# Attention value products as two half-height products each, on one core

## The chip, the core and the metric

The kernel runs on one core of a Trainium2 chip. Its measure is the device time of one execution in microseconds. The matrix unit (TensorE, in the profile PE for products and PEld for loads of the stationary operand) takes the products; VectorE (DVE), ScalarE (ACT) and GpSimd (POOL) do the rest; SyncE (SP) issues the DMAs. Products land in PSUM, which has eight banks of 512 float32 columns in each of 128 partitions.

## The reference, cut to what is computed

```python
B, S, D, H, F = 1, 2048, 576, 32, 4608
xn = layernorm(x)                                   # no weights
q, k, v = split((xn @ wqkv), heads=32)              # 18 columns a head
p = softmax(q @ k.T * 18 ** -0.5)                   # 32 heads of 2048 x 2048
s = concat(p @ v) @ wo
g = silu((gelu(xn @ w_gate) * (xn @ w_up)) @ w_down)
out = x + s * g
```

Everything is float32. The products p @ v are the value products of this document.

## The kernel before, in words

A prologue normalises x and projects q, k and v into DRAM. Then one long loop runs attention and the feed-forward part side by side, and an epilogue applies `wo` and the gate. Most products take their operands as float32r (a high and a low part, several terms a product); the value products are plain float32, and the profile shows each of them as two loads and two products.

**Units.** Attention is cut into 128 sections. Four sections make one of `NU` = 32 units: a unit is four heads (`QD`) against one block of 512 queries (`TB`), and its section c takes keys of chunk c, 512 of them, as four tiles of 128 keys (kt). A section has first a mixed part: 27 pairs of gate and up products (`gate_up`, line 420), one of a pair in each half of the array's rows, so 64 rows each, and between them eight slots. A slot has a score pair of the current unit (`score_pair`, line 887, result `pe`), of which ScalarE makes exponentials into `pT` (line 888), and a pair for the maxima of the next unit (`max_pair`, line 846, result `pm`), which VectorE reduces (line 847, `mx`). Both are pairs of 64-row products too.

**Values.** Behind the mixed part `values` runs for the section's four key tiles (line 904). For each tile there are four products, one a head: 128 keys in rows, 32 columns of the stationary operand `VS` (18 values and a column of ones that gives the sum of the exponentials, the rest unused), 512 queries moving. The four heads lie in four column strips of the array, 32 wide, and land in four strips of 32 partitions of one bank. Chunk 0's result is copied into `accs` in SBUF by ScalarE (line 908); those of chunks 1, 2 and 3 are added to it by VectorE (line 910). After chunk 3 `accs` goes to DRAM, and a later section divides by the sums.

**Behind the values.** Behind chunk 2 of a unit VectorE ends the next unit's maxima (`max_parts`: `neg` of line 855, `mt` of line 858) and takes a reciprocal (line 935), and the next mixed part begins. Behind chunk 0 the next mixed part begins at once. Behind chunks 1 and 3 come the down products of the feed-forward part (`halved`, line 518, result `py`, 64-row pairs as well), which VectorE adds into `M` (line 568); then the next mixed part.

**PSUM.** All results of the loop share one ring of four tiles of two banks (`ring`, `RING` = 4). A section's `pgu` keeps one tile through its mixed part. The other three go round in the order of the program, so `pe` and `pm` take the tile of the third result before them: a `pm` takes that of the `pe` one slot before, a `pe` that of the `pm` two slots before, and the second `pe` of a section that follows values directly takes the tile of `acc`. A value result uses one of its tile's two banks.

**Order.** The order on TensorE is written out by hand (`spread` puts the slots between the pairs), as is SP's. VectorE, ScalarE and GpSimd are ordered by the scheduler in the loop, apart from instructions marked to stay in program order. Each engine runs its own list in order.

The epilogue's `project` (line 1059) and last down products (line 581) are products of 128 rows and 128 columns; between them lie gate and up pairs of 64 rows.

Of the kernel before, what the change touches and what calls it, by code (L numbers as in the profile page):

```python
# [8 lines left out]
F32 = mybir.dt.float32  # L9
F32R = mybir.dt.float32r  # L10
AF = mybir.ActivationFunctionType
ALU = mybir.AluOpType
# [5 lines left out]
P = 128  # L18
NT = S // P
TB = 512  # L20
# [3 lines left out]
HR = 64  # L24
# [3 lines left out]
QD = 4  # L28
# [5 lines left out]
NA = NS // SLOTS  # L34
VC = NT // NA
KB, VB = 7, 2
# [27 lines left out]
def part(b, r):  # L64
    return r if b != 1 or r > PLAIN else r - 1 if r > 0 else PLAIN
# [6 lines left out]
def f(ap):  # L72
    return ap.bitcast(F32)
# [14 lines left out]
def kernel(ctx: ExitStack, tc: tile.TileContext, x, wqkv, wo, w_gate, w_up, w_down, out):  # L88
    nc = tc.nc
# [83 lines left out]
    with tc.tile_pool(name="pro", bufs=1) as pro, tc.tile_pool(name="pps", bufs=1, space=PSUM) as pps:  # L173
# [120 lines left out]
        def split_qk(t, raw):  # L294
            hi, lo = (pro.tile([P, KT, P], F32R, name=f"q{m}{t}") for m in "hl")
            first = split(hi, lo, raw)
            put_qk(t, hi, lo)
            return first
# [31 lines left out]
        t = ORDER[0]  # L330
# [15 lines left out]
        last = norm(xr, 0, True, first_loads)  # L346
# [8 lines left out]
        for b in range(NB):  # L355
            if b == NB - 1:
                tc.keep_in_program_order(nc.scalar.activation(eps, eps, AF.Tanh))
            for n, t in enumerate(ORDER):
# [4 lines left out]
                if b == 0 and ahead_qk:  # L363
                    first = split_qk(*ahead_qk.pop(0))
# [40 lines left out]
    def ring(name):  # L405

        return ps.tile([P, 2, TB], F32, name=name, tag="ring", bufs=RING)
# [310 lines left out]
    def at(n, part, what, *args):  # L718
        todo.setdefault((n, part), []).append(lambda: what(*args))
# [66 lines left out]
    with tc.tile_pool(name="att", bufs=1, reuse_waits="tile") as att:  # L786
        VS = [att.tile([P, VC * VW + 32 - DH - 1], F32, name=f"VS{i}") for i in range(VB)]
# [36 lines left out]
        QS, MX, ACC, SUM, PT, NM, DEN = {}, {}, {}, {}, {}, {}, {}  # L824
# [12 lines left out]
        def max_pair(u, i):  # L837

            if u not in MX:
                MX[u] = att.tile([P, QD, 4, 4], F32, name="mx", bufs=2)  # L840
            i, r = divmod(i, 2)
            c, t = divmod(i, 4)
            pm = ring("pm")
            for a in range(2):
                rr = slice(HR * a, HR * a + HR)
                nc.tensor.matmul(pm[:, a], QS[u, r][rr, t * P:(t + 1) * P], KS[(u * NA + c) % KB][r][rr, :], start=True, stop=True)  # L846
            nc.vector.tensor_reduce(MX[u][:, 2 * r:2 * r + 2, t, c], pm, axis=AX.X, op=ALU.max)  # L847
# [4 lines left out]
        def max_parts(u):  # L852

            keep = tc.keep_in_program_order
            keep(nc.vector.tensor_reduce(NEG[:, 0].rearrange("p (a r t) -> p a r t", a=2, r=2),
                                         MX[u].rearrange("p (r a) t c -> p a r t c", a=2), axis=AX.X, op=ALU.max, negate=True))
            mt = att.tile([P, 8 * QD], F32, name="mt", bufs=2)
            keep(nc.vector.transpose(mt, NEG.rearrange("p z c -> p (z c)")))
            hl = NM[u] = att.tile([P, 2, 8 * QD], F32R, name="mhl", bufs=2)
            nc.scalar.activation(hl[:, 0], mt, AF.Copy)  # L860
            nc.gpsimd.tensor_tensor(hl[:, 1], mt, f(hl)[:, 0], op=SUB)
            FF["parts"] = True
            for i, part in ((9, max_store), (18, max_end)):
                FF["hooks"].setdefault(i, []).append(lambda part=part: part(u))
# [25 lines left out]
        def slot_pairs(s):  # L890

            um, im = divmod(s + LEAD, NS)
            return [lambda: score_pair(*divmod(s, NS))] + [lambda: max_pair(um, im)] * (um < NU)

        def values(u, kt):
            j, g = divmod(u, NQ)
            first, last = kt % VC == 0, kt % VC == VC - 1
            if first:
                ACC[u] = ring("acc")[:, 0]
            pt = PT.pop((u, kt))  # L900
            for a in range(QD):
                c, t = divmod(kt, VC)
                v = t * VW + (DH + 1) * a
                nc.tensor.matmul(ACC[u][32 * a:32 * a + 32, :], VS[(u * NA + c) % VB][:, v:v + 32], pt[:, a, :],  # L904
                                 start=first, stop=last, skip_group_check=True)
            if last and kt < VC:
                SUM[u] = att.tile([P, TB], F32, name="accs")
                nc.scalar.activation(SUM[u], ACC.pop(u), AF.Copy)
            elif last:
                nc.vector.tensor_tensor(SUM[u], ACC.pop(u), SUM[u], op=ALU.add)  # L910
            if kt == NT - 1:
                cols = slice(j * TB, (j + 1) * TB)
                acc = SUM[u]
                at(u * NA + NA - 1, 1, nc.sync.dma_start, oT[g, :, cols], acc)
                rt = rT[QD * g:QD * (g + 1), cols]
                if u < NU - 1:
                    todo.setdefault(((u + 1) * NA, 0), []).insert(0, lambda: sums(u, rt))
                    at((u + 1) * NA + 2, 2, reciprocals, u, rt)
                else:
                    at(NU * NA - 1, 2, last_sums, u, rt)  # L920

        def sums(u, rt):
            j, g = divmod(u, NQ)
            den = DEN[u] = att.tile([P, QD * TB // P], F32, name="sums", bufs=2)
            nc.sync.dma_start(den, oT[g].rearrange("(a p) t -> a p t", p=32)[:, 0, j * TB:(j + 1) * TB]
                              .rearrange("a (c s) -> a c s", s=QD * TB // P))
# [12 lines left out]
        for n, m in enumerate(FIRST):  # L939
            none = [lambda: None]  # L940
            lead = [lambda s=s: max_pair(*divmod(s, NS)) for s in range(slot, slot + m)]
            if m:
                lead = 5 * none + lead if n == 2 else 2 * none + lead + none
            section(lead)
            if slot + m >= NS > slot:
                max_parts(0)
            slot += m
            while n > 0 and chunk < KB and chunk * SLOTS <= slot + SLOTS:
                load_k(chunk)
                chunk += 1  # L950
            if n == 0:
                load_k(0)
                load_q(0)
            if n == 3:
                load_q(1)
            if n >= len(FIRST) - 2:
                load_v(n - len(FIRST) + 2)
            downs()
            finish()
        scaled = gated = 0  # L960
        later = {}
        for n in range(NU * NA):
            u, i = divmod(n, NA)
# [19 lines left out]
            for kt in range(i * SLOTS // 2, (i + 1) * SLOTS // 2):  # L983
                values(u, kt)
            if im == 0 and um <= NU:
                max_parts(um - 1)
# [11 lines left out]
    with tc.tile_pool(name="epi", bufs=1, reuse_waits="tile") as epi:  # L998
# [141 lines left out]
        first = FF["n"]  # L1140
# [27 lines left out]
        last = FF["raw"].pop(first + 4)  # L1168
# [9 lines left out]
        for m in ("rawd", "tsum"):  # L1178
            t = ffn.tile([P, 2, D], F32, name="xxs", tag=m)
# [34 lines left out]
        for i, c, m in QUARTERS:  # L1214
            t = ffn.tile([P, 2, DC], F32, name="tg", tag=("h0", "h1")[c], bufs=2 - c)
# [34 lines left out]
```

## Time and profile before

| | |
|---|---|
| median of 3 runs | 2528.89 us (2528.62 to 2529.62) |
| profiled execution, its own time | 2528.7 us |
| its span, first to last instruction | 2526.9 us |
| granted TensorE clock | 1.00 |
| TensorE busy | 2520.1 us (100%) |
| VectorE, ScalarE, GpSimd busy | 1890.4, 1666.2, 1599.4 us |
| value products on TensorE (line 904) | 466.0 us, 4096 of them |
| the loop with the values | from 317 to 2408 us of the span |

A row of a group gives the line, the engine, the operation, the tiles out<-in, the shapes and the count, then busy time in us and the mean of one in ns, then the idle time of that engine just before and who ended it. `64*128 64x512` is a stationary operand of 64 rows and 128 columns with 512 columns moving. A row of the timeline gives the start and the length in us of one or, with x2, of several instructions merged; a bracket at its end tells for how long the engine had been idle and who ended that. Lengths of products include what is in the pipeline, so it is the distance of starts that tells how fast they follow each other.

### The profile page before, as it was taken

The numbers are of one execution on the slowest core, as the hardware profiler recorded it, in microseconds if no ns is written. First come the engines' busy times: TensorE is split into PE (matmuls) and PEld (weight loads), VectorE is DVE, ScalarE is ACT, GpSimd is POOL, SyncE is SP. The second block draws the span as 40 slices with busy tenths as digits, with TensorE's granted clock in tenths as the row PEclk, the third lists the DMA queues.
The fourth block names the chain that finished last, engine by engine and source line by source line (L and its number), as shares of the span: only waits on it lengthen the run. The fifth ranks groups of instructions, "written<-read, shape, count | busy, mean of one in ns | idle before, by whom it ended". The sixth has DMA issues, their size and how long they took to land.

```text
span 2526.9 us, 58757 instructions
## 1 busy us (share of the span) xinstructions
PE 2520.1 (100%) x23434; PEld 1827.4 (72%) x23434; DVE 1890.4 (75%) x2085; ACT 1666.2 (66%) x1889; POOL 1599.4 (63%) x1652
## 2 busy tenths in 40 slices
PE   9999999999999999999999999999999999999999
PEld 8888866666766677666667666676666676666789
DVE  5326788888888888888887888888887788888247
ACT  3223377778777776777777777677777777777731
POOL 3005688888888875666657556566667666666773
PEclk9999999999999999999999999999999999999999
DMA  8965456555585566666677666666668666665766
GB/s 262 313 206 139 120 173 170 153 168 164 170 246 155 165 177 151 167 163 168 169 218 191 175 174 166 169 170 163 156 162 244 167 173 173 172 164 153 190 186 243
DMA packets 416649, 455.40 MB, mean 180 GB/s; under 512 B 109428, under 2 KB 289396, under 8 KB 416376
## 3 DMA queue, kind: packets, MB, share of 16 engines
q1 hardware_dynamic: 416376, 451.64, 65.1%
q8 instruction: 186, 3.05, 0.5%
q14 instruction: 87, 0.71, 0.1%
HBM read 354.38 MB, written 97.13 MB: 179 GB/s over the span
## 4 chain that ended last, share of the span: by engine, by line
PE 97%; DMA 2%; DVE 1%; POOL 0%; issue 0%; SPq 0%; ACT 0%; POOLq 0%; DVEq 0%
PE pgu L420 35%; PE acc L904 18%; PE py L518 16%; PE pm L846 10%; PE pe L887 9%; PE po L194 7%; PE po L1059 1%; DMA raw<-in_B_w_up_dram 1%; PE py L581 1%; PE pt L264 0%; DMA rT<-rec 0%; DMA xx<-in_A_wo_dram 0%; DMA T<-ts 0%; DMA xx<-in_A_x_dram 0%; DVE ol L1042 0%
## 5 line engine op out<-in xcount | busy, mean ns | idle before, releaser
L888 ACT ACTIVATE pT<-pe 128x1024 f32<-128x1024 f32 x1024 | 1048.6, 1027 | 469.4 <-PE pe L887 435.6
L847 DVE TENSOR_REDUCE mx<-pm 128x2 f32<-128x1024 f32 x1024 | 1218.7, 1226 | 143.9 <-PE pm L846 128.8
L420 PE MATMUL pgu<-xd,wh 64*128 64x512 f32 x5184 | 958.5, 393 | 0.0
L420 PEld LDWEIGHTS pgu<-xd,wh 64*128 64x128 f32 x5184 | 496.2, 184 | 122.5 <-issue 41.6
L118 POOL TENSOR_SCALAR wh<-raw 128x384 fp32r<-128x384 f32 x402 | 208.5, 519 | 506.7 <-PE pgu L420 264.0
L420 PE MATMUL pgu<-xd,wl 64*128 64x512 f32 x2592 | 514.4, 390 | 0.2 <-POOL wl L120 0.2
L904 PE MATMUL acc<-pT,VS 128*32 128x512 f32 x4096 | 466.0, 595 | 0.0
L120 POOL TENSOR_TENSOR wl<-raw,wh 128x384 fp32r<-128x384 f32 x402 | 407.4, 1014 | 33.0
L846 PE MATMUL pm<-KA,QT 64*128 64x512 f32 x2048 | 411.9, 396 | 0.2 <-DVE mx L847 0.2
L887 PE MATMUL pe<-QT,KA 64*128 64x512 f32 x2048 | 408.1, 391 | 0.0
L518 PE MATMUL py<-T,ah 64*128 64x288 f32 x3848 | 389.8, 294 | 0.0
L568 DVE TENSOR_TENSOR M<-py,M 128x576 f32<-128x576 f32 x448 | 333.2, 756 | 54.7 <-PE py L518 39.9
L518 PEld LDWEIGHTS py<-T,ah 64*128 64x128 f32 x3848 | 317.6, 184 | 53.2 <-issue 52.8
L441 POOL TENSOR_TENSOR al<-h,ah 128x512 fp32r<-128x512 f32 (+1 forms) x143 | 295.6, 2067 | 49.2 <-ACT ah L438 24.0
L904 PEld LDWEIGHTS acc<-pT,VS 128*32 128x32 f32 x4096 | 120.0, 109 | 276.9 <-issue 229.8
L518 PE MATMUL py<-T,al 64*128 64x288 f32 x1924 | 294.9, 291 | 0.0
L420 PEld LDWEIGHTS pgu<-xd,wl 64*128 64x128 f32 x2592 | 247.6, 184 | 46.6 <-POOL wl L120 0.6
L887 PEld LDWEIGHTS pe<-QT,KA 64*128 64x128 f32 x2048 | 192.9, 184 | 112.0 <-DVE mx L847 12.5
L432 DVE TENSOR_TENSOR h<-h,pgu 128x512 f32<-128x512 f32 x139 | 95.6, 687 | 194.2 <-ACT h L429 190.1
L846 PEld LDWEIGHTS pm<-KA,QT 64*128 64x128 f32 x2048 | 195.1, 184 | 55.5 <-ACT pT L888 15.8
L518 PEld LDWEIGHTS py<-T,al 64*128 64x128 f32 x1924 | 192.2, 185 | 0.0
L429 ACT ACT_TABLE_LOAD x129 | 165.5, 1283 | 2.4
(151 smaller groups left out, 2138.4 us busy)
## 6 DMA issues: line engine op xcount, KB each, us to landing
T<-ts SPq DMA_DIRECT2D x98, 576.0 KB
KA<-qk SPq DMA_DIRECT2D x768, 72.0 KB
T<-ts SPq DMA_DIRECT2D x98, 432.0 KB
raw<-in_B_w_gate_dram SPq DMA_DIRECT2D x144, 288.0 KB
raw<-in_B_w_up_dram SPq DMA_DIRECT2D x144, 256.0 KB
ts<-T SPq DMA_DIRECT2D x36, 576.0 KB
VS<-vs SPq DMA_DIRECT2D x128, 152.0 KB
qk<-t SPq DMA_DIRECT2D x72, 256.0 KB
```

The source lines that it names most:

```text
L118: first = nc.gpsimd.tensor_scalar(hi, raw, 1.0, 1.0, op0=ALU.mult, op1=ALU.mult)
L120: keep(nc.gpsimd.tensor_tensor(lo, raw, f(hi), op=ALU.subtract))
L194: nc.tensor.matmul(o, st, m, start=(i == 0), stop=(i == len(terms) - 1))
L420: nc.tensor.matmul(o, w[1 + wp][k][rr, c, :], xd[k][xp][rr, c, :], start=(i == 0), stop=(i == len(terms) - 1))
L441: low = two.tensor_tensor(lo, raw, f(hi), op=ALU.subtract)
L518: one = nc.tensor.matmul(py[:, t, 0:DC], h[rr, a, t * P:(t + 1) * P], T[rr, w, k], start=x == 0 and n == 0, stop=x == 1 and n == len(terms ...
L568: nc.vector.tensor_tensor(M[:, m], py[:, :, 0:DC], M[:, m], op=ALU.add)
L846: nc.tensor.matmul(pm[:, a], QS[u, r][rr, t * P:(t + 1) * P], KS[(u * NA + c) % KB][r][rr, :], start=True, stop=True)
L847: nc.vector.tensor_reduce(MX[u][:, 2 * r:2 * r + 2, t, c], pm, axis=AX.X, op=ALU.max)
L887: nc.tensor.matmul(pe[:, a], KS[(u * NA + c) % KB][r][rr, t * P:(t + 1) * P], QS[u, r][rr, :], start=True, stop=True)
L888: nc.scalar.activation(PT[u, kt][:, 2 * r:2 * r + 2, :], pe, AF.Exp, scale=SCALE)
L904: nc.tensor.matmul(ACC[u][32 * a:32 * a + 32, :], VS[(u * NA + c) % VB][:, v:v + 32], pt[:, a, :], start=first, stop=last, skip_group_chec ...
```

## The change

Each value product is cut in two: rows 0 to 63 of the keys and rows 64 to 127, each a product of 64 rows in its half of the array (`HR` = 64). The first half sums into the first bank of the ring tile, the second half into the second bank, so `acc` uses both banks and the array tile is 64x32 where it was 128x32. `accs` holds both sums, 1024 columns. Chunk 0 copies both at once on ScalarE; chunks 1 and 2 add both at once on VectorE. At the first key tile of chunk 3 VectorE joins the two sums in SBUF into one, and at chunk 3's end it adds the two banks to it, one after the other. To make room in SBUF, the maxima (`mx`) and their parts (`mhl`) have one buffer in place of two.

```diff
-                MX[u] = att.tile([P, QD, 4, 4], F32, name="mx", bufs=2)
+                MX[u] = att.tile([P, QD, 4, 4], F32, name="mx")
...
-            hl = NM[u] = att.tile([P, 2, 8 * QD], F32R, name="mhl", bufs=2)
+            hl = NM[u] = att.tile([P, 2, 8 * QD], F32R, name="mhl")
...
             if first:
-                ACC[u] = ring("acc")[:, 0]
+                ACC[u] = ring("acc")
+            if kt == NT - VC:
+                nc.vector.tensor_tensor(SUM[u][:, 0], SUM[u][:, 0], SUM[u][:, 1], op=ALU.add)
             pt = PT.pop((u, kt))
+            c, t = divmod(kt, VC)
             for a in range(QD):
-                c, t = divmod(kt, VC)
                 v = t * VW + (DH + 1) * a
-                nc.tensor.matmul(ACC[u][32 * a:32 * a + 32, :], VS[(u * NA + c) % VB][:, v:v + 32], pt[:, a, :],
-                                 start=first, stop=last, skip_group_check=True)
+                for half in range(2):
+                    rr = slice(HR * half, HR * half + HR)
+                    nc.tensor.matmul(ACC[u][32 * a:32 * a + 32, half], VS[(u * NA + c) % VB][rr, v:v + 32], pt[rr, a, :],
+                                     start=first, stop=last, skip_group_check=True)
             if last and kt < VC:
-                SUM[u] = att.tile([P, TB], F32, name="accs")
+                SUM[u] = att.tile([P, 2, TB], F32, name="accs")
                 nc.scalar.activation(SUM[u], ACC.pop(u), AF.Copy)
+            elif last and kt < NT - 1:
+                nc.vector.tensor_tensor(SUM[u], ACC.pop(u), SUM[u], op=ALU.add)
             elif last:
-                nc.vector.tensor_tensor(SUM[u], ACC.pop(u), SUM[u], op=ALU.add)
+                SUM[u], acc = SUM[u][:, 0], ACC.pop(u)
+                for half in range(2):
+                    nc.vector.tensor_tensor(SUM[u], acc[:, half], SUM[u], op=ALU.add)
```

## The prediction, as it was put on record

> **What bounds the kernel now.** I read the page first: busy shares, the chain of work that ended last, and the costliest groups.
>
> ```profile
> PE 2520.1 (100%) x23434; PEld 1827.4 (72%) x23434; DVE 1890.4 (75%) x2085; ACT 1666.2 (66%) x1889; POOL 1599.4 (63%) x1652
> ...
> PEclk9999999999999999999999999999999999999999
> ...
> PE 97%; DMA 2%; DVE 1%; POOL 0%; issue 0%; SPq 0%; ACT 0%; POOLq 0%; DVEq 0%
> PE pgu L420 35%; PE acc L904 18%; PE py L518 16%; PE pm L846 10%; PE pe L887 9%; PE po L194 7%; PE po L1059 1%; DMA raw<-in_B_w_up_dram 1%; PE py L581 1%; PE pt L264 0%; DMA rT<-rec 0%; DMA xx<-in_A_wo_dram 0%; DMA T<-ts 0%; DMA xx<-in_A_x_dram 0%; DVE ol L1042 0%
> ...
> L904 PE MATMUL acc<-pT,VS 128*32 128x512 f32 x4096 | 466.0, 595 | 0.0
> ```
>
> TensorE is the bound at full clock: 97% of the chain, and the value products (line 904) are 18% of it. So I went to the timeline of TensorE around one of their 128 runs, which shows where time in them is not streaming.
>
> ```profile
> 1209.77 0.41 PE L846 MATMUL pm<-KA,QT 64*128 64x512 f32 x2
> 1210.01 0.42 PE L420 MATMUL pgu<-xd,wh 64*128 64x512 f32 x2
> 1210.35 3.64 PE L904 MATMUL acc<-pT,VS 128*32 128x512 f32 x32
> 1213.92 0.50 PE L420 MATMUL pgu<-xd,wh 64*128 64x512 f32 x2
> 1214.26 0.39 PE L887 MATMUL pe<-QT,KA 64*128 64x512 f32 x2
> 1214.49 0.39 PE L420 MATMUL pgu<-xd,wl 64*128 64x512 f32 x2
> ```
>
> A pair of 64-row products normally starts 0.23 to 0.24 us after the pair before (1209.77 to 1210.01, 1214.26 to 1214.49). Into the values it is 0.34, out of the values the second pair is at 0.34 too (1213.92 to 1214.26). Inside the run, the weight loads and the length of one product give the rounds:
>
> ```profile
> 1210.81 0.13 PEld L904 LDWEIGHTS acc<-pT,VS 128*32 128x32 f32 x4 [0.30 <-issue]
> 1211.24 0.13 PEld L904 LDWEIGHTS acc<-pT,VS 128*32 128x32 f32 x4 [0.30 <-issue]
> ...
> L904 PE MATMUL acc<-pT,VS x4096: 592/592/617, 317.0 to 2408.0; 128*32 128x512 f32 x196
> ```
>
> The run ends at 1213.99 and its last product lasts 0.592, so that one starts at 1213.40. Four heads work side by side, a round takes 0.43 (1210.81 to 1211.24), and 32 products make eight rounds. After the last round the next pair would be due at 1213.40 - 0.02 + 0.43 = 1213.81; it starts at 1213.92. So one trip into the values and back costs 0.10 at the entry, 0.02 in the first round (its products are those of 617 ns instead of 592), 0.11 at the exit and 0.11 at the pair behind: 0.34 us, 43.5 us over 128 trips. That is all the change can gain on TensorE.
>
> Is this price one of the rows or of the columns? Only rows change at two places near the end, to 128x128 products and back:
>
> ```profile
> 2462.24 0.39 PE L420 MATMUL pgu<-xd,wl 64*128 64x512 f32 x2
> 2462.47 0.39 PE L420 MATMUL pgu<-xd,wh 64*128 64x512 f32 x2
> 2462.79 0.40 PE L1059 MATMUL po<-woh,oh 128*128 128x288 f32 x1
> 2463.03 0.30 PE L1059 MATMUL po<-wol,oh 128*128 128x288 f32 x1
> 2463.16 0.29 PE L1059 MATMUL po<-woh,ol 128*128 128x288 f32 x1
> ...
> 2449.62 0.29 PE L1059 MATMUL po<-wol,KA 128*128 128x288 f32 x1
> 2449.84 0.50 PE L420 MATMUL pgu<-xd,wh 64*128 64x512 f32 x2
> 2450.18 0.40 PE L420 MATMUL pgu<-xd,wl 64*128 64x512 f32 x2
> ```
>
> In: 0.32 instead of 0.23, then 0.24 instead of 0.13. Back: 0.22 instead of 0.13, then 0.34 instead of 0.23. That is 0.09 + 0.11 + 0.09 + 0.11 = 0.40 for a trip where rows alone change, not less than the 0.34 where rows and columns change at once.
>
> **The change part by part.** *Two products of 64 rows for each of 128.* A tile of 64x32 replaces one of 128x32; eight work side by side where four did. The pairs of halves in the rows above show that halves run beside each other: two products of 64 rows and 512 columns in 0.23. So I take a round as 0.43 still, eight rounds a run. From below it is that; from above, halves one after the other, eight rounds more, 128 x 8 x 0.43 = +440 us. The starts of one round are (0.13 - 0.109)/3 = 0.007 apart (load of 109 ns in the page's group of these loads, quoted below), so four more tiles in the last round let the next pair in 0.028 later: 128 x 0.028 = +3.6 us.
>
> *The switch.* Rows stay at 64 now, columns still go from 128 to 32 and back. No row of the trace shows a change of columns alone, so it costs between 0 and 0.34 a trip. The nearest rows are the two kinds of trip above: that a double change costs no more than a single one looks like one emptying of the array for any change of shape, not like a price of rows with columns free. I take the full 0.34: nothing gained. The Trainium skill, "TensorEngine Tiling (Array Packing)", under Key Properties, says that a change of the tiling mode, as against the tile, drains TensorE, and its list of configurations has 64x128 and 64x32 as two modes. By that rule the sum stays as I have it; the other reading is the first rival, and no run here shows a change of columns alone.
>
> *Emptying two banks.* Rows for the prices:
>
> ```profile
> L904 PEld LDWEIGHTS acc<-pT,VS 128*32 128x32 f32 x4096 | 120.0, 109 | 276.9 <-issue 229.8
> L910 DVE TENSOR_TENSOR accs<-acc,accs x96: 690/693/694, 334.5 to 2408.7; 128x512 f32<-128x512 f32 x96
> L568 DVE TENSOR_TENSOR M<-py,M 128x576 f32<-128x576 f32 x448 | 333.2, 756 | 54.7 <-PE py L518 39.9
> L888 ACT ACTIVATE pT<-pe 128x1024 f32<-128x1024 f32 x1024 | 1048.6, 1027 | 469.4 <-PE pe L887 435.6
> ```
>
> From 512 to 576 elements VectorE's add grows by 0.064 us, 0.001 an element, so an add of 1024 is 0.69 + 0.53 = 1.22 us. ScalarE's copy of 1024 is 1.03 as for the exponential of that size, against 0.60 for 512 (quoted below): +0.43. What this moves differs by chunk, of which a unit has four; there are 32 units.
>
> Chunk 2 is the dear one. VectorE's queue behind its add, and who waits for it:
>
> ```profile
> 1214.06 0.69 DVE L910 TENSOR_TENSOR accs<-acc,accs 128x512 f32<-128x512 f32 x1 [0.86 <-PE acc L904]
> 1214.67 0.21 DVE L855 TENSOR_REDUCE neg<-mx 128x16 f32<-128x64 f32 x1
> ...
> 1215.18 4.90 DVE L847 TENSOR_REDUCE mx<-pm 128x2 f32<-128x1024 f32 x4
> ...
> 1216.46 0.19 PEld L887 LDWEIGHTS pe<-QT,KA 64*128 64x128 f32 x2 [0.17 <-DVE mx L847]
> 1216.57 0.40 PE L887 MATMUL pe<-QT,KA 64*128 64x512 f32 x2
> ```
>
> The first reduction of the next section starts as soon as this queue lets it, at 1215.18, and takes 1.23. Of the four ring tiles one is held by pgu; the other three go round, so the third pe takes the tile of the first pm and its weight load follows that reduction's end (1216.41) by 0.05. With 0.53 more in front the reduction ends at 1216.94, the load is at 1216.99 and the product between 1217.00 (together with its load, as at 1213.92) and 1217.10 (0.11 behind it, as here): +0.43 to +0.53, I take 0.50. The products come in one order, so everything behind shifts and nothing wins it back.
>
> Chunk 0 is emptied by ScalarE:
>
> ```profile
> 1247.13 0.60 ACT L908 ACTIVATE accs<-acc 128x512 f32<-128x512 f32 x1
> ...
> 1247.83 2.12 ACT L888 ACTIVATE pT<-pe 128x1024 f32<-128x1024 f32 x2
> ...
> 1248.95 0.19 PEld L846 LDWEIGHTS pm<-KA,QT 64*128 64x128 f32 x2
> 1249.18 0.39 PE L846 MATMUL pm<-KA,QT 64*128 64x512 f32 x2
> ```
>
> The copy ends at 1248.16 instead of 1247.73, the first exponential 1.03 later at about 1249.19 instead of 1248.86. The second pm has that pe's tile: its load comes at 1249.24, the product at 1249.25 to 1249.35 instead of 1249.18: +0.07 to +0.17, I take 0.12.
>
> Behind chunks 1 and 3 the down products come, and VectorE has a gap before it adds the first:
>
> ```profile
> 1227.79 0.69 DVE L910 TENSOR_TENSOR accs<-acc,accs 128x512 f32<-128x512 f32 x1 [0.84 <-PE acc L904]
> 1229.15 3.14 DVE L568 TENSOR_TENSOR M<-py,M 128x576 f32<-128x576 f32 x4 [0.67 <-PE py L518]
> ```
>
> The 0.67 covers chunk 1's +0.53. Chunk 3's second add of 0.69 ends 0.02 late, which the four adds win back (3.14 for 4 x 0.756 = 3.02). If that cover went, the 0.53 and 0.69 would cost 39 us. The join of the two sums, one add of 512 (about 0.7), stands at the start of chunk 3's values, in front of the 0.84 that VectorE waits there. Nothing. The store of the sums through SP's queue leaves up to 0.7 later; what reads it back is taken a section later, at no price. One buffer in place of two for the maxima and their parts: their reader stands ahead of the next writer on VectorE already (1214.67 before 1215.18). Nothing.
>
> **Sum.** 32 x (0.50 + 0.12) + 3.6 = 23.4 us. The profiled execution took 2528.7 us (span 2526.9), 0.2 below the median of the runs shown, so 2552 us.
>
> **The rivals.** *Columns are free, rows were the price* (the other side). For it: every costly trip in the trace changes rows. Against: a double change costs no more than a single one. Place: both ends of each run of values. Gain in a unit: the entry, 4 x 0.12 = 0.48, and the exits behind chunks 1 and 3, 2 x 0.22 = 0.44. The exits behind chunks 0 and 2 bring nothing, since the waits there hang on the emptying, which counts from the end of the values. Against 0.62 + 4 x 0.028 = 0.73, net -0.19 x 32 = -6 us: 2523. It decides from four fifths of the price saved (0.73 of 0.92).
>
> *The switch gets cheaper by half*: -0.46 + 0.73 = +0.27 a unit, +9 us: 2538.
>
> *Columns free and the emptying hidden* (VectorE put the maxima before the adds): -43.5 + 3.6: 2489. Against: the queue order shown, in which the add is ready 1.1 us before the first maximum.
>
> *TensorE is not fed fast enough.* A round now has eight loads and eight products in 0.43. The densest stretch of today:
>
> ```profile
> 1228.14 0.44 PE L518 MATMUL py<-T,ah 64*128 64x288 f32 x4
> 1228.40 0.31 PE L518 MATMUL py<-T,al 64*128 64x288 f32 x2
> 1228.54 0.44 PE L518 MATMUL py<-T,ah 64*128 64x288 f32 x4
> ```
>
> Six products in 0.40, 0.066 each. Were that the limit of issue, a round would take 0.53: 8 x 128 x 0.10 = +102, and 2654 with the sum above. Against it: single 128x128 products of 288 columns also take 0.13 (2463.03 to 2463.16), so columns set that pace, not issue. The Trainium skill, "TensorE: Matmul & The Clock Gate", Part 1, gives about 62 ns a matmul when firmware decodes; by it a round would be an estimated 0.50, no run here tells how this chip decodes.
>
> **How the numbers follow.** Full price 0.44, half 0.10, columns free 0.30, free and hidden 0.09, fed too slowly (or halves one after another) 0.07. Range 2514 to 2560 leaves out the last two, 0.16. Its upper end is the full price with waits of 0.53 and 0.17 (2555) and 5 us for what I rounded, its lower end columns free with 0.43 and 0.07 (2519) and the same 5 us. The likeliest case alone spans 2544 (0.43, 0.07, no later start) to 2560. A measurement of this kernel tells about 0.2% (5 us) from nothing. Columns free lies at that edge: two thirds faster (0.21), with free and hidden 0.30. Same: the rest, and a little of half, 0.12. Slower 0.58.
>
> **What would show it.** Right: the first pair behind the values still 0.34 before the second; the entry still 0.34; eight rounds of 0.43; add 1.22 and copy 1.03; behind chunk 2 a weight load of the third pe that waits 0.4 to 0.6 for a maximum. Wrong: pairs at 0.23 on both sides of the values (columns free), rounds above 0.45 (feed), or maxima ahead of the adds on VectorE.

## The result, and the profile after

The changed kernel takes 2566.25 us (median of 4 runs) against 2529.26 for the kernel before: ratio 1.0145, 95% interval 1.0127 to 1.0163. It is slower, as forecast, by 37 us where 23 were forecast, and it lies 6 us above the range.

The page after, line by line against the one before (busy shares, the chain, the value products' group, then who keeps `pe` waiting):

```profile
PE 2536.7 (99%) x27530; PEld 1842.8 (72%) x27530; DVE 1959.2 (76%) x2149; ACT 1673.9 (65%) x1889; POOL 1599.7 (62%) x1652
...
PE 95%; DVE 4%; issue 1%; DMA 0%; ACT 0%; SPq 0%; DVEq 0%
PE pgu L420 33%; PE acc L908 18%; PE py L518 15%; PE pm L846 9%; PE pe L887 9%; PE po L194 7%; PE po L1067 2%; DVE accs L914 1%; DVE mx L847 1%; PE py L581 1%; PE pt L264 0%; DVE mt L858 0%; DVE accs L901 0%; DMA KA<-qk 0%; DMA xx<-in_A_x_dram 0%
...
L908 PE MATMUL acc<-pT,VS 64*32 64x512 f32 x8192 | 469.0, 592 | 0.0
...
L887 PE MATMUL pe<-QT,KA 64*128 64x512 f32 x2048 | 408.7, 396 | 21.4 <-DVE mx L847 21.4
```

Twice as many value products take 469.0 us of TensorE's time, where half as many took 466.0: eight tiles run beside each other, in rounds of 0.429 us as before. What is new is VectorE in the chain (4%, where it was 1%) with the lines of the emptying, the join (L901) and the maxima, and 21.4 us in which TensorE stands idle for a maximum. Before, the same row of `pe` had none:

```profile
L887 PE MATMUL pe<-QT,KA 64*128 64x512 f32 x2048 | 408.1, 391 | 0.0
```

The timeline of TensorE behind one chunk 2, after:

```profile
1225.14 0.40 PE L846 MATMUL pm<-KA,QT 64*128 64x512 f32 x2
1225.37 0.40 PE L420 MATMUL pgu<-xd,wh 64*128 64x512 f32 x2
1225.70 3.66 PE L908 MATMUL acc<-pT,VS 64*32 64x512 f32 x64
1229.30 0.49 PE L420 MATMUL pgu<-xd,wh 64*128 64x512 f32 x2
1229.63 0.40 PE L887 MATMUL pe<-QT,KA 64*128 64x512 f32 x2
...
1232.82 0.50 PE L887 MATMUL pe<-QT,KA 64*128 64x512 f32 x2 [0.63 <-DVE mx L847]
1233.15 0.39 PE L420 MATMUL pgu<-xd,wl 64*128 64x512 f32 x2
```

The entry is 0.33 (1225.37 to 1225.70), the second pair 0.33 behind the first (1229.30 to 1229.63): the price of the trip is all there, though rows no longer change. From the first value product to the first pair behind is 3.60, where it was 3.57: the later end of eight tiles. And the third `pe` of the section comes 3.52 after the first pair; before it was 2.65 (1213.92 to 1216.57). Behind its wait the next pair is 0.33 away as well (1232.82 to 1233.15), 0.10 more than usual.

To see where the 37 us lie, I took the distance from each run of values to the next and subtracted that of the kernel before, for the 32 units, by the chunk that stands ahead (median of one, and the sum):

| behind chunk | 0 | 1 | 2 | 3 |
|---|---|---|---|---|
| changed kernel, us each | +0.11 | +0.03 | +1.00 | +0.03 |
| sum, us | 3.5 | 0.8 | 32.6 | 1.5 |

The sum is 38.4, and the spans differ by 38.2 (2565.1 and 2526.9). Chunks 0, 1 and 3 did what the prediction said. Behind chunk 0 it is also the second `pm` that waits, for an exponential behind ScalarE's longer copy:

```profile
1263.59 1.03 ACT L912 ACTIVATE accs<-acc 128x1024 f32<-128x1024 f32 x1
...
1265.58 0.19 PEld L846 LDWEIGHTS pm<-KA,QT 64*128 64x128 f32 x2 [0.25 <-ACT pT L888]
```

Chunk 2 lost twice as much. VectorE's timeline there shows why:

```profile
1229.47 1.23 DVE L914 TENSOR_TENSOR accs<-acc,accs 128x1024 f32<-128x1024 f32 x1 [0.91 <-PE acc L908]
1230.61 0.21 DVE L855 TENSOR_REDUCE neg<-mx 128x16 f32<-128x64 f32 x1
1230.74 0.68 DVE L901 TENSOR_TENSOR accs<-accs 128x512 f32<-128x512 f32 x1
1231.34 0.20 DVE L858 STREAM_TRANSPOSE mt<-neg 128x32 f32<-128x32 f32 x1
1231.47 0.21 DVE L943 RECIPROCAL sums<-sums 128x16 f32<-128x16 f32 x1
1231.60 2.29 DVE L847 TENSOR_REDUCE mx<-pm 128x2 f32<-128x1024 f32 x2
```

The join L901, written at the start of chunk 3's values, does not run there. The scheduler, which orders VectorE in the loop, put it between `neg` and `mt`, one section earlier, where chunk 2's add has already made its operand. So two things stand ahead of the first maximum: the longer add (+0.53) and the join. The join takes 0.60 of the queue (1230.74 to 1231.34), but `mt` would have started only 0.24 behind `neg` without it (as in the next kernel below) and starts 0.73 behind it now, so it adds 0.49. The maximum starts 2.13 after the add (1229.47 to 1231.60), where it was 1.12, and the third `pe` waits for its end.

### The profile page after: what moved, and what is told of

Read it like the earlier page. It is cut to its first block, busy times and chain, and to the rows that moved or that the text cites. A ratio compares the mean times of both kernels' runs of the same rounds, so it can differ in the third digit from the quotient of the medians.

```text
span 2565.1 us, 67100 instructions
## 1 busy us (share of the span) xinstructions
PE 2536.7 (99%) x27530; PEld 1842.8 (72%) x27530; DVE 1959.2 (76%) x2149; ACT 1673.9 (65%) x1889; POOL 1599.7 (62%) x1652
## 3 DMA queue, kind: packets, MB, share of 16 engines
q8 instruction: 218, 3.57, 0.6%
## 4 chain that ended last, share of the span: by engine, by line
PE 95%; DVE 4%; issue 1%; DMA 0%; ACT 0%; SPq 0%; DVEq 0%
PE pgu L420 33%; PE acc L908 18%; PE py L518 15%; PE pm L846 9%; PE pe L887 9%; PE po L194 7%; PE po L1067 2%; DVE accs L914 1%; DVE mx L847 1%; PE py L581 1%; PE pt L264 0%; DVE mt L858 0%; DVE accs L901 0%; DMA KA<-qk 0%; DMA xx<-in_A_x_dram 0%
## 5 line engine op out<-in xcount | busy, mean ns | idle before, releaser
L908 PE MATMUL acc<-pT,VS 64*32 64x512 f32 x8192 | 469.0, 592 | 0.0
L887 PE MATMUL pe<-QT,KA 64*128 64x512 f32 x2048 | 408.7, 396 | 21.4 <-DVE mx L847 21.4
L120 POOL TENSOR_TENSOR wl<-raw,wh 128x384 fp32r<-128x384 f32 x402 | 407.5, 1014 | 33.3
L518 PEld LDWEIGHTS py<-T,ah 64*128 64x128 f32 x3848 | 309.5, 185 | 52.9 <-issue 52.8
L908 PEld LDWEIGHTS acc<-pT,VS 64*32 64x32 f32 x8192 | 141.3, 106 | 258.5 <-issue 211.5
L518 PE MATMUL py<-T,al 64*128 64x288 f32 x1924 | 285.9, 291 | 0.0
L518 PEld LDWEIGHTS py<-T,al 64*128 64x128 f32 x1924 | 184.0, 185 | 0.0
```

The source lines that it names most:

```text
L120: keep(nc.gpsimd.tensor_tensor(lo, raw, f(hi), op=ALU.subtract))
L518: one = nc.tensor.matmul(py[:, t, 0:DC], h[rr, a, t * P:(t + 1) * P], T[rr, w, k], start=x == 0 and n == 0, stop=x == 1 and n == len(terms ...
L887: nc.tensor.matmul(pe[:, a], KS[(u * NA + c) % KB][r][rr, t * P:(t + 1) * P], QS[u, r][rr, :], start=True, stop=True)
L908: nc.tensor.matmul(ACC[u][32 * a:32 * a + 32, half], VS[(u * NA + c) % VB][rr, v:v + 32], pt[rr, a, :], start=first, stop=last, skip_group ...
```

## The experiments

My theory after the result: a change of columns costs the full trip, and the rest is VectorE's queue ahead of the first maximum, half of it the misplaced join. The rivals are that something else in the change makes the loss (the single buffer of the maxima, the `acc` tile held longer, the 64-row products), or that columns are cheap and the emptying hides it. The kernel before, run beside them, takes 2529.86 us for the first four kernels and 2529.7 for the last two. "By chunk" is the loss of one section against the kernel before, as in the table above, behind chunks 0, 1, 2 and 3.

**The join where its line stands.** The join is held behind the last maximum of chunk 3's section (`behind` tells the scheduler the order of two instructions).

```diff
-            nc.vector.tensor_reduce(MX[u][:, 2 * r:2 * r + 2, t, c], pm, axis=AX.X, op=ALU.max)
+            FF["reduced"] = nc.vector.tensor_reduce(MX[u][:, 2 * r:2 * r + 2, t, c], pm, axis=AX.X, op=ALU.max)
...
-                nc.vector.tensor_tensor(SUM[u][:, 0], SUM[u][:, 0], SUM[u][:, 1], op=ALU.add)
+                behind(nc.vector.tensor_tensor(SUM[u][:, 0], SUM[u][:, 0], SUM[u][:, 1], op=ALU.add), FF["reduced"])
```

> The changed kernel with the join of the two sums held behind the last maximum of chunk 3's section, where its line stands in the text. My theory: of the 1.00 us lost behind each chunk 2, about half is the join, which the scheduler put between neg and mt, in front of the first maximum; the rest is the add's 0.53. So behind chunk 2 the loss falls from 1.00 to about 0.50, all else stays (0.11 behind chunk 0, 0.03 behind 1 and 3): 2529 + 32 x (0.50 + 0.11 + 0.06) = about 2550 us. Rival: the loss is made by the single buffer of the maxima and their parts, or by the acc tile that the second pe waits for; then 1.00 stays and the time is 2566.

Measured: 2549.87 us, ratio 1.0079 (1.0066 to 1.0091). By chunk +0.12, +0.02, +0.53, +0.03. VectorE behind chunk 2, and the third `pe`'s load:

```profile
1222.57 1.22 DVE L914 TENSOR_TENSOR accs<-acc,accs 128x1024 f32<-128x1024 f32 x1 [0.90 <-PE acc L908]
1223.71 0.21 DVE L855 TENSOR_REDUCE neg<-mx 128x16 f32<-128x64 f32 x1
1223.95 0.21 DVE L858 STREAM_TRANSPOSE mt<-neg 128x32 f32<-128x32 f32 x1
1224.09 0.21 DVE L943 RECIPROCAL sums<-sums 128x16 f32<-128x16 f32 x1
1224.21 2.29 DVE L847 TENSOR_REDUCE mx<-pm 128x2 f32<-128x1024 f32 x2
...
1225.43 0.19 PEld L887 LDWEIGHTS pe<-QT,KA 64*128 64x128 f32 x2 [0.58 <-DVE mx L847]
```

The first maximum now starts 1.64 after the add, and the join is hidden. One instruction's place in a queue is worth 16 us of the 37. The single buffers are still there, so they are not the cause of these 16. This kernel is the change as I had costed it; its time is 2 us below my 2552.

**The end of the maxima ahead of chunk 2's values.** In addition, `max_parts` is called before the values and not behind them.

```diff
+            if im == 0 and um <= NU:
+                max_parts(um - 1)
             for kt in range(i * SLOTS // 2, (i + 1) * SLOTS // 2):
                 values(u, kt)
-            if im == 0 and um <= NU:
-                max_parts(um - 1)
```

> The kernel late_join with the end of the next unit's maxima (neg, mt) put ahead of chunk 2's values, so that they run while VectorE waits for the values. The add of 1024 columns stays as long as it is. My theory (what counts is only what stands in VectorE's queue between the values' end and the first maximum): the first maximum starts about 0.15 later than in the kernel before instead of 0.53, the loss behind chunk 2 falls to 0.1 to 0.2, and the time is 2529 + 32 x (0.15 + 0.11 + 0.06) = about 2539 us. Rival (the acc tile is held longer, and the second pe waits for it): the add ends at the same time as in late_join, so the loss stays about 0.5 and the time is 2550.

Measured: 2540.37 us, ratio 1.0042 (1.0029 to 1.0055). By chunk +0.12, +0.02, +0.18, +0.03.

```profile
1217.51 0.21 DVE L855 TENSOR_REDUCE neg<-mx 128x16 f32<-128x64 f32 x1
1217.76 0.21 DVE L858 STREAM_TRANSPOSE mt<-neg 128x32 f32<-128x32 f32 x1
1218.50 1.23 DVE L914 TENSOR_TENSOR accs<-acc,accs 128x1024 f32<-128x1024 f32 x1 [0.53 <-PE acc L908]
1219.64 0.24 DVE L943 RECIPROCAL sums<-sums 128x16 f32<-128x16 f32 x1
1219.80 4.84 DVE L847 TENSOR_REDUCE mx<-pm 128x2 f32<-128x1024 f32 x4
```

The add is as long as before and ends as late behind the values (1.33 behind the end of the last value product in both kernels, median), so the `acc` tile is held as long; yet most of the loss is gone, since the first maximum starts 1.30 after the add and not 1.64. The second `pe`'s load does wait for the tile, but for the same 0.23 in the kernel with only the join late (the first row) and in this one (the second):

```profile
1223.85 0.19 PEld L887 LDWEIGHTS pe<-QT,KA 64*128 64x128 f32 x2 [0.23 <-DVE accs L914]
...
1219.78 0.19 PEld L887 LDWEIGHTS pe<-QT,KA 64*128 64x128 f32 x2 [0.23 <-DVE accs L914]
```

So what made the difference is the queue ahead of the maximum, not the hold of the tile.

**Chunk 0 by two engines.** In addition, ScalarE copies the first bank and VectorE the second.

```diff
-                nc.scalar.activation(SUM[u], ACC.pop(u), AF.Copy)
+                nc.scalar.activation(SUM[u][:, 0], ACC[u][:, 0], AF.Copy)
+                nc.vector.tensor_copy(SUM[u][:, 1], ACC.pop(u)[:, 1])
```

> The kernel late_join_early_max with chunk 0 emptied by two engines at once, ScalarE the first bank and VectorE the second. My theory: ScalarE's copy takes 0.60 again, so the 0.08 that chunk 0 loses beyond the later start of eight tiles goes: 2 to 3 us less than late_join_early_max, about 2536 us, and what is left over the kernel before is the later end of eight tiles, 128 x 0.03. Rival (the change of columns is cheaper than I think and the emptying hid it): with the emptying hidden the time falls below the kernel before, to 2520 or less.

Measured: 2542.99 us, ratio 1.0052 (1.0039 to 1.0064): slower than the kernel before it by 2.6, not faster by 2 to 3. Behind chunk 0 it loses 0.19 where that lost 0.12. The timeline behind one chunk 0, ScalarE, VectorE and the loads:

```profile
1253.50 0.60 ACT L912 ACTIVATE accs<-acc 128x512 f32<-128x512 f32 x1
...
1254.13 0.69 DVE L913 COPY accs<-acc 128x512 f32<-128x512 f32 x1 [1.54 <-ACT accs L912]
...
1254.87 0.19 PEld L887 LDWEIGHTS pe<-QT,KA 64*128 64x128 f32 x2 [0.33 <-DVE accs L913]
```

The two copies do not run at once: VectorE's waits for ScalarE's (1.54 idle, ended by the ACT line), though it reads another bank. The tile is then free at 1254.82, and the second `pe`, which takes it, waits for that. My expectation was wrong in this step. The two copies share the ring tile that they read and the `accs` tile that they write; which of the two orders them, no run here shows. As the emptying is not hidden behind chunk 0, this kernel is no test of cheap columns there. Behind chunks 1 and 3, where the emptying costs nothing in any of these kernels, cheap columns would have been a gain, and the sections lose 0.03 as in the others.

**One bank emptied.** All 64-row products run, but the second half's sums and the join are left out.

```diff
-            if kt == NT - VC:
-                nc.vector.tensor_tensor(SUM[u][:, 0], SUM[u][:, 0], SUM[u][:, 1], op=ALU.add)
...
-                SUM[u] = att.tile([P, 2, TB], F32, name="accs")
-                nc.scalar.activation(SUM[u], ACC.pop(u), AF.Copy)
-            elif last and kt < NT - 1:
-                nc.vector.tensor_tensor(SUM[u], ACC.pop(u), SUM[u], op=ALU.add)
+                SUM[u] = att.tile([P, TB], F32, name="accs")
+                nc.scalar.activation(SUM[u], ACC.pop(u)[:, 0], AF.Copy)
             elif last:
-                SUM[u], acc = SUM[u][:, 0], ACC.pop(u)
-                for half in range(2):
-                    nc.vector.tensor_tensor(SUM[u], acc[:, half], SUM[u], op=ALU.add)
+                nc.vector.tensor_tensor(SUM[u], ACC.pop(u)[:, 0], SUM[u], op=ALU.add)
```

> The changed kernel's products, but only the first bank is emptied: the second half's sums are left out, and the join with them. TensorE does all that the changed kernel does, VectorE and ScalarE what the kernel before does. My theory: the products cost only the later end of eight tiles, 128 x 0.03, so 2529 + 4 = about 2533 us. Rival A (columns free, hidden by the emptying): 2490 to 2520. Rival B (64-row products of plain float32 or their second bank slow other work): above 2538.

Measured: 2534.11 us, ratio 1.0016 (1.0007 to 1.0025): 4.2 us. By chunk +0.05, +0.03, +0.05, +0.03. On TensorE the change gains nothing and costs little more than the later end of eight tiles. So 33 of the 37 us are the emptying and the join.

**Values without a change of shape.** On top of it, a section's values are products of 64x128 tiles: as many rounds, one head's worth of products in place of four, other columns of `VS`.

```diff
-            for a in range(QD):
-                v = t * VW + (DH + 1) * a
-                for half in range(2):
-                    rr = slice(HR * half, HR * half + HR)
-                    nc.tensor.matmul(ACC[u][32 * a:32 * a + 32, half], VS[(u * NA + c) % VB][rr, v:v + 32], pt[rr, a, :],
-                                     start=first, stop=last, skip_group_check=True)
+            for half in range(2):
+                rr = slice(HR * half, HR * half + HR)
+                nc.tensor.matmul(ACC[u][:, half], VS[(u * NA + c) % VB][rr, 0:P], pt[rr, t, :],
+                                 start=first, stop=last, skip_group_check=True)
```

> The kernel one_bank, but a section's values are products of 64 rows and 128 columns, the shape of all other products of the loop: one head's worth of moving columns for each key tile and half, so eight rounds again with two tiles side by side instead of eight. It leaves out three heads in four and takes other columns of VS, so the sums are others; the rounds, the waits and the emptying stay. My theory: the whole trip price (0.34) is a change of shape, columns alone included. Without it the entry saves 0.12 each time, the exits behind chunks 1 and 3 save 0.22, those behind 0 and 2 about 0.1 (waits for the first exponential and the first maximum, which count from the values' end): 32 x (0.48 + 0.44 + 0.2) = 36 us below one_bank plus the 4 us of eight tiles: about 2493 us (2485 to 2505). Rival: the price belongs to the values themselves (plain float32 in two passes, or the wait for pT), not to the shape: entry and exit stay at 0.33 and the second pair at 0.33, about 2530.

Measured: 2491.81 us, ratio 0.9853 (0.9838 to 0.9868): 42 us below the kernel of one bank, 38 below the kernel before. TensorE's timeline around one run of values:

```profile
1357.21 0.40 PE L846 MATMUL pm<-KA,QT 64*128 64x512 f32 x2
1357.45 0.40 PE L420 MATMUL pgu<-xd,wh 64*128 64x512 f32 x2
1357.68 3.60 PE L904 MATMUL acc<-pT,VS 64*128 64x512 f32 x16
1360.71 0.80 PE L420 MATMUL pgu<-xd,wh 64*128 64x512 f32 x2
1361.35 0.40 PE L887 MATMUL pe<-QT,KA 64*128 64x512 f32 x2
1361.58 0.41 PE L420 MATMUL pgu<-xd,wl 64*128 64x512 f32 x2
```

The entry is 0.23 now, as between any two pairs. The run is nearly as long (3.60 against 3.66), still eight rounds of plain float32 in two passes, behind the same exponentials; and the second pair behind the values stands 3.90 after the entry's pair (1357.45 to 1361.35), where with 64x32 tiles it is 4.26 (1225.37 to 1229.63). The first pair behind is recorded 0.02 behind the last round's products (1360.69) and lasts 0.80 where 0.40 is usual; with 0.43 for that last round it would be due at 1361.12, and the second pair stands 0.23 behind that. So the exit has no price left either. By chunk, against the kernel before: -0.31, -0.34, -0.22, -0.33, which is the trip price of 0.34 of the prediction, less where the first maximum or the first exponential holds the section up. So columns alone, 64x32 among 64x128, cost the whole price. The number of tiles in a round changes with the columns here, from eight to two, and this kernel can't separate them; but four tiles of 128x32 paid 0.34 at the entry and eight of 64x32 0.33, so the price doesn't go with the number. The Trainium skill, "TensorEngine Tiling (Array Packing)", Key Properties, has the rule that a change of tiling mode drains TensorE; the traces now fit it for columns too, with 0.33 at the entry in place of 0.23, though they show the delay and not the drain itself.

**The join alone.** The kernel of one bank with an add of 512 columns in SBUF at the join's line (to itself).

```diff
+            if kt == NT - VC:
+                nc.vector.tensor_tensor(SUM[u], SUM[u], SUM[u], op=ALU.add)
             pt = PT.pop((u, kt))
```

> The kernel one_bank with an add of 512 columns in SBUF (accs to itself, so its sums are others) where the join stands in the text; the scheduler puts it between neg and mt as in the changed kernel. The add out of PSUM has 512 columns. My theory: it delays the first maximum by 0.60 and the third pe by 0.45 to 0.60 behind each chunk 2, nothing elsewhere: 14 to 19 us above one_bank, about 2549 us. Rival (only the longer hold of the acc tile counts): as one_bank, about 2533.

Measured: 2547.22 us, ratio 1.0071 (1.0058 to 1.0084): 13 us above the kernel of one bank, just under the 14 to 19 I gave. By chunk +0.05, +0.03, +0.47, +0.03. VectorE behind a chunk 2:

```profile
1221.92 0.69 DVE L914 TENSOR_TENSOR accs<-acc,accs 128x512 f32<-128x512 f32 x1 [0.91 <-PE acc L908]
1222.53 0.21 DVE L855 TENSOR_REDUCE neg<-mx 128x16 f32<-128x64 f32 x1
1222.66 0.68 DVE L901 TENSOR_TENSOR accs<-accs 128x512 f32<-128x512 f32 x1
1223.26 0.20 DVE L858 STREAM_TRANSPOSE mt<-neg 128x32 f32<-128x32 f32 x1
1223.39 0.21 DVE L939 RECIPROCAL sums<-sums 128x16 f32<-128x16 f32 x1
1223.51 2.29 DVE L847 TENSOR_REDUCE mx<-pm 128x2 f32<-128x1024 f32 x2
```

The maximum starts 1.59 after the add, where it was 1.12. With the add out of PSUM short and the tile free as early as before, the misplaced join alone makes a loss behind chunk 2, and there only.

**All of them by one measure.** For 30 units of each kernel I read how long after the end of chunk 2's values the first maximum ends, and subtracted the kernel before's 2.42 (median); beside it stands the loss behind chunk 2:

| kernel | first maximum ends later by, us | loss behind chunk 2, us |
|---|---|---|
| changed | 0.98 | 1.00 |
| join late | 0.50 | 0.53 |
| join late, maxima early | 0.16 | 0.18 |
| one bank emptied | 0.01 | 0.05 |
| join alone | 0.44 | 0.47 |

The loss is the delay of the first maximum and 0.02 to 0.04 more, which is about the later end of eight tiles.

## Why the prediction was wrong, point by point

- *The switch at its full price*: right. Entry and second pair stayed at 0.33, and the kernel without a change of shape shows that columns alone carry it. The first rival, columns free, falls.
- *Rounds of 0.43, eight tiles side by side, TensorE fed fast enough*: right (469.0 us in all; eight products in 0.429 are 0.054 each, under the 0.066 of the rival that feared for the feed). *The later end, 0.028 a section*: right, +0.03 behind chunks 1 and 3, 4.2 us in all where 3.6 were put.
- *Chunk 0, +0.12 by ScalarE*: right in kind, 0.08 in size (0.11 less the 0.03 of the later end), within its bounds.
- *Chunk 2, +0.50 by the add*: right. With the join elsewhere the loss is 0.53, later end included.
- *The join, "Nothing"*: the step that failed. I took the line's place in the text for its place in VectorE's queue and named the 0.84 of idle time as its cover. But VectorE is ordered by the scheduler in the loop, as the description of the kernel says, and nothing tied the join to chunk 3. It went ahead of the first maximum, and the 0.49 that it added to the queue made it about as dear as the add: 16 us by the kernel with the join late. I named no price for that case. The working held one, since anything of that length ahead of the maximum costs about what the add costs: 0.50 x 32 = 16 us, and 2568 in all.
- *The single buffers and the store, nothing*: right as far as seen: with the single buffers in place the kernel with the late join loses only what the add and the later end explain, and the kernel of one bank loses 0.05 behind chunk 2.

No version here that does the whole computation beats the kernel before: without a gain on TensorE there is nothing that the emptying of a second bank could be paid from.

## What to carry to other kernels

Cutting products so that their rows match the neighbours' buys nothing while their columns still differ: in these traces a trip to another tile shape and back cost 0.34 to 0.40 us whether rows, columns or both changed, and only equal shapes saved it. Before an added instruction is costed at nothing, look up who orders its engine; if a scheduler does, an instruction that is ready early can land ahead of the one everything waits for, so cost it there or pin it. In a loop where one engine's reduction frees the other's buffer, look at the length of the queue between the last product and the first reduction: here it set the loss, while the engine's busy share (VectorE was at 75%) told nothing of it.

## What the runs showed of the hardware that I had not expected

The join's length varies, and the emptying's does not (the adds of 1024 columns last 1.223 to 1.226 in the changed kernel). From the changed kernel's view by source line, the join:

```profile
L901 DVE TENSOR_TENSOR accs<-accs x32: 683/683/1533, 355.4 to 2436.7; 128x512 f32<-128x512 f32 x32
```

All four of its 32 that lasted over 1.0 us had GpSimd's subtraction of line 120 running beside them, such as the one at 1836.97 (VectorE's rows first, GpSimd's below):

```profile
1835.71 1.23 DVE L914 TENSOR_TENSOR accs<-acc,accs 128x1024 f32<-128x1024 f32 x1 [0.91 <-PE acc L908]
...
1836.97 1.48 DVE L901 TENSOR_TENSOR accs<-accs 128x512 f32<-128x512 f32 x1
...
1835.32 1.01 POOL L120 TENSOR_TENSOR wl<-raw,wh 128x384 fp32r<-128x384 f32 x1
...
1836.89 1.01 POOL L120 TENSOR_TENSOR wl<-raw,wh 128x384 fp32r<-128x384 f32 x1
```

The join starts 0.08 behind GpSimd's and ends 0.80 later than the usual 0.68 would have it. Behind that chunk 2 the section lost 1.83 and not 1.00. The Trainium skill, "SBUF — State Buffer", Who interferes with whom, says that a VectorE instruction with two inputs in SBUF contends with a GpSimd instruction that reads SBUF. The trace agrees: the join has both inputs in SBUF; the add of `accs`, one of whose inputs is in PSUM, takes its 1.23 here too, beside another L120 (1835.32).

The runs show more than that one case. Of the changed kernel's 32 joins 26 had no GpSimd instruction beside them, and all of these took 0.683 or 0.684. The kernel with the late join moves the join to a place where GpSimd is at work in all but one of the units:

```profile
L901 DVE TENSOR_TENSOR accs<-accs x32: 684/1086/2276, 365.2 to 2419.1; 128x512 f32<-128x512 f32 x32
...
1234.06 1.09 DVE L901 TENSOR_TENSOR accs<-accs 128x512 f32<-128x512 f32 x1
...
1233.32 1.28 POOL L745 TENSOR_TENSOR on<-on,od 128x512 f32<-128x512 f32 x1
```

In both kernels every join that began while a GpSimd instruction ran (6 and 31 of them) ended 0.55 us behind that instruction's end, however long the two had run side by side (0.14 to 1.73 us). That looks as if the join stood nearly still until GpSimd's instruction was through. Behind chunk 2 this costs time, and in the late place it is hidden.
